# A gated mix of a spectral filter and a squared-relu MLP, forward and backward: ScalarE's order in the opening, and one plain block instead of two in the output pass

## The chip, the core and the metric

The kernel runs on one core of a Trainium2 chip. The core has a matrix engine (TensorE; PE in the profile, PEld its weight loads), a vector engine (VectorE, DVE), a scalar engine (ScalarE, ACT), GpSimd (POOL) and SyncE (SP). Each takes its own instructions in order and waits for others by semaphores. In this kernel SP issues most loads, POOL issues stores and a few loads. The metric is the device time of one execution in microseconds; lower is better. A "profiled execution" is one run recorded by the hardware profiler; its span is the time from the first to the last instruction.

## What is computed

The reference computes an output and, for a given `grad_out`, the gradients of all inputs:

```python
g = sigmoid((x * gate_w).sum(-1, keepdims=True))      # x: 2048 x 1024
a = irfft2(rfft2(x) * (w_r + 1j * w_i))               # spectral branch
b = relu(x @ w1 + b1) ** 2 @ w2 + b2                  # MLP, F = 3584
out = g * a + (1 - g) * b
# and the vjp of this with grad_out, for x, w_r, w_i, w1, b1, w2, b2, gate_w
```

## The kernel before

The matrix work runs in three stages, and a "side" (the two-dimensional transforms of the spectral branch, forward and backward, as small TensorE products with VectorE and ScalarE work around them) is spread between their units.

1. `mlp_in`: for each pair of hidden column blocks and each 512 rows, `hidden` makes `ph` = x w1 (eight matmuls of 128x512), a relu (`rT`, line 748) and its square (`h2T`, line 749) on ScalarE; `grads` makes `pd` = (scaled `grad_out`) w2 transposed (eight matmuls, line 755) and the product with the relu on VectorE (line 759). `h2T` and `dhT` go to DRAM. `ph` and `pd` use few PSUM banks in turn, so a chain can only start when the reader of an earlier one is done.
2. `mlp_grads`: the gradients of w1 and w2.
3. `mlp_out`: the product of the squared relu with w2 (the output rows) and then of `dhT` with w1 (the gradient of x), in blocks of 256 rows.

**The opening.** The first 32 units of stage 1 are written out by a loop (lines 1745 to 1758): units 0 to 7 and 16 to 23 run `hidden`, the others `grads`, and between them tiles of x and of the gradient are transposed (`turn_x`, `turn_grad`) and the gate is made. `weigh` (line 666) gives the row sums `gsum` of one tile of 128 rows on VectorE, as soon as its rows have landed; `gate(i0)` makes the two sigmoids `omg` (1 - g) and `gcol` (g) of four tiles on ScalarE and scales four tiles of the gradient `dbn` by `omg` on VectorE. `gate(12)`, the last, is called after unit 19. From unit 21 on each odd unit takes one step of the side's first stage (`first_stage_of_x`). Its `folds` takes sums and differences of a row on VectorE and copies a few edge elements on ScalarE (lines 263, 265, 269); `row_stage` is the small product `pk`.

The order in which a program's lines are written is not yet the order on an engine: a scheduler sets it from dependencies and its own estimates. `after(ins, earlier, wait)` adds a dependency; with `NoSync` it only fixes the order of two instructions of one engine, with `Sync` (the default) it makes the later one wait.

**The output pass.** `cL` and `cR` are the left and right halves (512 columns each) of w2, 28 blocks of 128 rows; `cL` (tile `w2L`) is loaded earlier, `cR` (tile `w2R`) by seven `rows_of_w2` loads at its start. A block k of 256 rows of the squared relu is loaded by `load("h", k)` into tile `even` or `odd`. A *plain* block makes four chains of 28 matmuls (two row halves by two column halves, tile `acc`, line 1475), each evicted by ScalarE. A *Winograd* block (class `Block`) makes the same by seven chains of 14 matmuls (`p1` to `p7`, line 1378), from sums of quarters: the left sums S1 to S4 of the block (`Block.sums`, VectorE, line 1374) and the right sums T1 to T4 of w2 (`w2_sums`, VectorE, line 1442), made once. Here `p6` reads S2 and T2, `p5` S1 and T1, `p7` S3 and T3, `p4` T4, `p3` S4.

Before, the first two blocks are plain (`N0 = 2`), in the order of `steps`, and blocks 2 to 7 are Winograd blocks. For each output row tile t, `fetch_a` and `fetch_g` load its spectral row and its row of `grad_out`; `prepare` scales the first on ScalarE (`na`) and adds the bias on VectorE (`v`); `close` joins and reduces on VectorE and scales on ScalarE, `put` subtracts and stores. These are kept in a fixed order per engine by `act` and `dve`. The last part of the side, `fft_out`, runs beside the first blocks: its folds (`rf`, VectorE) and copies (`re`, ScalarE) feed its product `pki`, whose result ScalarE copies (`rt`) for the product `pui`.

Of the kernel before, what the change touches and what calls it, by code (L numbers as in the profile page):

```python
# [10 lines left out]
P = 128  # L11
# [4 lines left out]
ACT = mybir.ActivationFunctionType  # L16
# [108 lines left out]
LEAD = 8  # L125
# [15 lines left out]
def kernel(  # L141
# [22 lines left out]
    nc = tc.nc  # L164
# [8 lines left out]
    R1, R2 = g.R1, g.R2  # L173
    NT = S // P
    Q, H, LW, W1 = D // 4, D // 2, g.Df + 1, g.Df
# [6 lines left out]
    ld, st = nc.sync.dma_start, nc.gpsimd.dma_start  # L182
# [7 lines left out]
    go_perm = gof.rearrange("(p t) d -> t p d", t=S2)  # L190
# [17 lines left out]
    gcol, omg, gpg, bGo, dsc = (cols(n, [NT]) for n in ("gcol", "omg", "gpg", "bGo", "dsc"))  # L208
    gsum = cols("gsum", [NT])
# [18 lines left out]
    ax_scr = [[dram.tile([P, D], FDT, name=f"ax_scr{T}_{i}") for i in range(NT)] for T in range(2)]  # L228
# [5 lines left out]
    def after(ins, earlier, wait=mybir.DependencyClass.Sync):  # L234

        if earlier is not None:
            info = mybir.DependencyInfo(wait, mybir.DependencyReason.DATA)
            tc.add_manual_dep(ins.ins, earlier.ins.name, info, reason="paced")


    turn = {"PE": None, "DVE": None, "ACT": None, "copy": None}
# [9 lines left out]
    tps, tps_s = pool("tps", "right", PSUM)  # L251


    def folds(fb, xt, earlier=None):
        uv = fb.tile([P, 2, H], FDT, name="uv", tag="uv", bufs=2)
        after(V(out=uv[:, 0, :], in0=xt[:, 0:H], in1=xt[:, H:D], op=ALU.add), earlier, mybir.DependencyClass.NoSync)
        after(V(out=uv[:, 1, :], in0=xt[:, 0:H], in1=xt[:, H:D], op=ALU.subtract), earlier, mybir.DependencyClass.NoSync)

        f = fb.tile([P, 6, Q + 2], FDT, name="f", tag="f", bufs=2)
        a0, a1 = uv[:, :, 1:Q], uv[:, :, H - 1 : Q : -1]  # L260
        V(out=f[:, 0:2, 1:Q], in0=a0, in1=a1, op=ALU.add)
        V(out=f[:, 2:4, 1:Q], in0=a0, in1=a1, op=ALU.subtract)
        nc.scalar.copy(out=f[:, 3:0:-2, 0], in_=uv[:, 1, 0 : Q + 1 : Q])

        nc.scalar.copy(out=f[:, 0:3:2, 0 : Q + 1 : Q], in_=uv[:, 0:1, 0 : Q + 1 : Q].to_broadcast([P, 2, 2]))
        b0, b1 = f[:, 0:3:2, 0:P], f[:, 0:3:2, Q:P:-1]
        V(out=f[:, 4:6, 0:P], in0=b0, in1=b1, op=ALU.add)
        V(out=f[:, 4:6, P:Q], in0=b0, in1=b1, op=ALU.subtract)
        nc.scalar.copy(out=f[:, 5, P::-P], in_=f[:, 0:3:2, P])
        return f  # L270
# [343 lines left out]

    def rows_of_w2(t_, fc, half, tie=None):
        src = B_w2[fc * P : (fc + 4) * P, half * H : (half + 1) * H]
        after(ld(out=t_[:, fc : fc + 4, :], in_=src.rearrange("(q p) e -> p q e", p=P)), tie)

    db_p, db_s = pool("db")
    dbn = db_p.tile([P, NT, D], BF16, name="dbn", tag="dbn")  # L620
# [4 lines left out]
    later = {}  # L625
    f1, f1_s = pool("f1", "right")

    cf = f1.tile(list(consts["cf"].shape), FDT, name="cf", tag="cf")
    xs = {}
# [42 lines left out]
    def gate(i0):  # L672

        c_ = slice(i0, i0 + 4)
        nc.scalar.activation(omg[:, c_], gsum[:, c_], ACT.Sigmoid, scale=-1.0)
        nc.scalar.activation(gcol[:, c_], gsum[:, c_], ACT.Sigmoid)
        for i in range(i0, i0 + 4):
            later["scaled"] = nc.vector.tensor_scalar(out=dbn[:, i, :], in0=dbn[:, i, :], scalar1=omg[:, i : i + 1], scalar2=None, op0=ALU.mult)
            after(later["scaled"], later["copied"], mybir.DependencyClass.NoSync)

    def first_stage_of_x():
        f, ft = {0: folds(f1, xs[0], later["last"])}, {}
        for i in range(NT + 1):
            if i + 3 < NT:
                xs[i + 3] = source(i + 3, x_perm, later["last"])
            if i < NT:
                ft[i] = row_stage(f1, f[i], kf[:], later["last"])
                yield
            if i > 0:
                first_columns(f1, cf, 0, i - 1, ft[i - 1], later["last"])  # L690
            if i + 1 < NT:
                f[i + 1] = folds(f1, xs[i + 1], later["last"])
            yield
# [23 lines left out]
    def mlp_in():  # L717
# [9 lines left out]
        def bank(name):  # L727
            drawn[0] += 1
            return banks[drawn[0] // 2 % len(banks)].tile([P, SW], FP32, name=name, tag="ph", bufs=2)
# [14 lines left out]
        def hidden(fc, ss, w1g, h2T, rT):  # L744
            ph = bank("ph")
            for dc in range(DC):
                opened(mm(ph[:], lhsT=w1g[:, dc, fc % 2 * P : (fc % 2 + 1) * P], rhs=xT[:, dc, ss], start=(dc == 0), stop=(dc == DC - 1)), fc)  # L747
            nc.scalar.activation(rT[:], ph[:], ACT.Relu, bias=b1col[:, fc : fc + 1])  # L748
            nc.scalar.activation(h2T, rT[:], ACT.Square)  # L749

        def grads(fc, sb, ss, rT, dhT):
            w_ = w2T[fc // FGC]
# [493 lines left out]
    def mlp_out():  # L1246
# [3 lines left out]
        cL, cR, spare = later["w2L"], wr.tile([P, FC, H], BF16, name="w2R", tag="w2R")[:], later["spare"]  # L1250
# [10 lines left out]
        a_, go, na, v, cu, ot, blks, halves = ({} for _ in range(8))  # L1261
# [11 lines left out]
        def load(which, k, issue=ld, tie=None):  # L1273
            t_ = later["odd" if k % 2 else "even"][:, 0 : FC * BW].rearrange("p (c b) -> p c b", b=BW)
            v_ = (h2T_scr if which == "h" else dhT_scr)[:].rearrange("c p s -> p c s")
            for h in (lo, hi):
                after(issue(out=t_[:, h, :], in_=v_[:, h, k * BW : (k + 1) * BW]), tie)
            blks[which, k] = t_
# [5 lines left out]

        def fetch_a(t):
            a_[t] = row("a_", FDT)
            ld(out=a_[t][:], in_=ax_scr[0][t][:])

        def fetch_g(t):
            go[t] = row("go3", BF16)  # L1290
            ld(out=go[t][:], in_=go_perm[t])

        def prepare(t):
            na[t], v[t] = row("na"), row("v")
            act(nc.scalar.mul(out=na[t][:], in_=a_.pop(t)[:], mul=-YS))
            dve(V(out=v[t][:], in0=na[t][:], in1=b2_bc, op=ALU.add))
# [163 lines left out]
            right(T4, cL[:, hi], T2)  # L1460

        blks["h", 0] = later["block"]
        N0 = 2
        fetch_a(0), fetch_g(0), fetch_a(1)
        fetch_g(1)
        made = w2_sums()
        load("h", 1, tie=later["tie"])
        for fc in range(0, FC, 4):
            rows_of_w2(cR, fc, 1)
        steps = [(0, 0), (1, 0), (2, 0), (0, 1), (1, 1), (2, 1), (3, 0), (3, 1)]  # L1470
        for t, hf in steps:
            k, t2 = divmod(t, 2)
            acc = mps.tile([P, H], FP32, name="acc", tag=("pX", "pV")[hf], bufs=2)
            for c in range(FC):
                turn["PE"] = mm(acc[:], lhsT=blks["h", k][:, c, t2 * P : (t2 + 1) * P], rhs=(cL, cR)[hf][:, c, :], start=(c == 0), stop=(c == FC - 1))
            act(nc.scalar.copy(out=fresh(t)[:, (L, R)[hf]], in_=acc[:]))
            turn["copy"] = turn["ACT"]
            if hf:
                if t:
                    put(t - 1)  # L1480
                if t + 1 < 2 * N0:
                    prepare(t + 1)
                close(t)
                fetch_a(t + 2)
                if t + 2 < 2 * N0:
                    fetch_g(t + 2)
                if t == 1:
                    load("h", 2)
            yield 2.0
            n = steps.index((t, hf))  # L1490
            if n == 2:
                prepare(0)
            if 3 <= n < 5:
                next(made)

        wq = iter(())
# [2 lines left out]
            yield from quarter(qs[0], 0, 0)  # L1499
            yield from quarter(qs[1], 0, 1)  # L1500

        a, b = None, Block("h", N0)
        b.sums(3, 1, 2)
        for k in range(N0, NB):
            last = k == NB - 1
            if k == NB - 3:
# [49 lines left out]
            a, b = b, Block("h", k + 1) if not last else Block("d", 0)  # L1556
# [51 lines left out]
        a, b = x1, None  # L1608
        for k in range(2, NB):
            last = k == NB - 1  # L1610
            b = Block("d", k)
# [26 lines left out]
            a = b  # L1638
        a.done = lambda t: close_x(t, ld)
        t_ = 2 * (NB - 1)  # L1640
        c_, v_, o_ = cu.pop(t_), v.pop(t_), row("gxo", BF16, tag="ot")
# [103 lines left out]
    for u in range(32):  # L1745
        for i in before.get(u, ()):
            turn_x(i)
        for i in grads_before.get(u, ()):
            turn_grad(i)
        next(units)  # L1750
        if u in (6, 15, 19):
            gate({6: 4, 15: 8, 19: 12}[u])
        if u == 17:
            for n in range(3):
                xs[n] = source(n, x_perm)
            stage = first_stage_of_x()
        if u > 19 and u % 2:
            next(stage)
    V(out=gpg[:], in0=gcol[:], in1=omg[:], op=ALU.mult)
    later["more_banks"]()  # L1760
# [42 lines left out]
        pass  # L1803
    grads = mlp_grads()
    next(grads), next(grads)
    total = 22 + 2 * (NT + 4) + 14 + 5 + 4 * R1 + 2 + LEAD + 4 * NT
    todo = total - 2 * 12

    def rate():
# [6 lines left out]
    for _ in spread(grads, spec, rate):  # L1816
        pass
    later["side"] = spec
    early = 8 * 2.0 + 3 * 7
    last_rate = (total - count[0]) / (early - 2.0)  # L1820
    for _ in spread(mlp_out(), spec, last_rate):
        pass
# [33 lines left out]
```

## Time and profile before

| | |
|---|---|
| times of four runs | 1205.83, 1207.93, 1207.95, 1210.36 us; median 1207.94 |
| the profiled execution | 1207.95 us, its span 1206.2 us |
| mean TensorE clock granted | 0.998 of full |
| DMA moved | 236.53 MB, mean 196 GB/s |
| TensorE waits in the whole span that the profile names | 4.9 us `ph` for `rT`; 2.0 (5 times) and 0.3 `pki` for `rf`; 1.5 `ph` for `w1g`; 1.2 `pz` for `zeros`; 1.2 `pki` for `re`; 0.5 `pV` for `gxo`; 0.2 `pX` for `u` |

How to read it: a line of a group names the source line, the engine, the operation, the tile written and the tiles read (`out<-in`), the count, then busy time and mean duration in ns, and after the bar the engine's idle time just before these instructions with what ended most of it. A line of a timeline gives start and duration in us, then the instruction, and in brackets the idle time before it and its releaser. `SPq` lines are issues of transfers on SP's queue; the duration is that of the issue, waits included. Matmuls follow each other faster than each one lasts: a group of eight of 128x512 has a duration of about 1.9 us at full clock.

### The profile page before, as it was taken

To read this page: it belongs to the slowest core of one execution; us is meant where nothing else is said; L and a number is where in the kernel's file an instruction comes from. 1 tells how busy PE (TensorE), PEld (TensorE's weight loads), DVE (VectorE), ACT (ScalarE), POOL (GpSimd) and SP (SyncE) were. 2 spreads that over 40 slices of the span, in tenths; PEclk is the share of its full clock that TensorE was granted. 3 is DMA by queue.
4 is the path that set the end of the run, shared out by engine and by line. 5 is a ranking of instruction groups with operands and counts; after the bars stand their busy time and mean duration, and the time that the engine had idled before them with its cause. 6 is when DMAs were issued, how large, how long until landed. Compare 5 with 4: busy or idle time off the path is not lost.

```text
span 1206.2 us, 19779 instructions
## 1 busy us (share of the span) xinstructions
PE 1183.0 (98%) x7055; PEld 648.4 (54%) x7149; DVE 845.3 (70%) x1842; ACT 615.4 (51%) x1121; POOL 366.0 (30%) x587
## 2 busy tenths in 40 slices
PE   9899999999999999999999999999999999999998
PEld 4455545544444444444447888888544544444444
DVE  5765646666879887877789856765489866966464
ACT  6147757855877873444444425554455523232322
POOL 1024424413455550433333353545132100000000
PEclk9999999999999999999999999999999999999999
DMA  9957566575757588999999799986876699965541
GB/s 263 287 170 195 148 201 192 159 171 177 204 175 208 184 224 177 181 213 225 220 201 179 179 234 173 218 199 195 280 215 178 197 206 251 251 194 173 160 150 35
DMA packets 341104, 236.53 MB, mean 196 GB/s; under 512 B 206237, under 2 KB 299963, under 8 KB 341004
## 3 DMA queue, kind: packets, MB, share of 16 engines
q1 hardware_dynamic: 309552, 144.08, 53.6%
q0 software_dynamic: 30224, 90.61, 24.2%
q8 instruction: 56, 0.92, 0.3%
q10 hardware_dynamic: 1228, 0.57, 0.2%
q14 instruction: 44, 0.36, 0.1%
HBM read 107.24 MB, written 81.81 MB: 157 GB/s over the span
## 4 chain that ended last, share of the span: by engine, by line
PE 86%; DVE 5%; DMA 4%; ACT 2%; issue 1%; SPq 1%; ACTq 0%; POOL 0%; DVEq 0%
PE pd L755 15%; PE ph L747 15%; PE pX L1378 13%; PE pV L1378 9%; PE pX L947 8%; PE pX L1023 6%; PE pV L947 6%; PE pV L1023 5%; PE pu L310 2%; PE pk L277 1%; PE px L416 1%; PE pv L447 1%; DMA odd<-h2T_scr 1%; DVE wT L1442 1%; DMA w2R<-in_B_w_dram 1%
## 5 line engine op out<-in xcount | busy, mean ns | idle before, releaser
L747 PE MATMUL ph<-xT,w1g 128*128 128x512 bf16 x867 | 215.8, 381 | 8.1 <-ACT rT L748 4.9
L755 PE MATMUL pd<-dbT,w2T 128*128 128x512 bf16 x876 | 209.5, 379 | 0.9
L755 PEld LDWEIGHTS <-w2T 128*128 128x128 bf16 x896 | 87.2, 98 | 102.8
L747 PEld LDWEIGHTS <-w1g 128*128 128x128 bf16 x896 | 85.7, 98 | 99.9 <-issue 6.8
L759 DVE SCALAR_TENSOR_TENSOR dhT<-pd,rT 128x512 bf16<-128x512 f32 x108 | 74.3, 688 | 77.7 <-PE pd L755 62.6
L748 ACT ACTIVATE rT<-ph,b1col 128x512 bf16<-128x512 f32 x108 | 74.6, 691 | 49.5 <-PE ph L747 46.8
L1023 PEld LDWEIGHTS <-res 128*128 128x128 bf16 (+1 forms) x896 | 86.8, 98 | 11.6 <-issue 0.6
L1378 PEld LDWEIGHTS <-dS 128*128 128x128 f16 x588 | 57.2, 98 | 66.0 <-issue 0.7
L226 POOL DMA_DIRECT2D r<-y_scr x96 | 58.6, 614 | 105.3 <-ACT re L553 57.9
L419 ACT CAST x<-px 64x512 f16<-64x512 f32 x128 | 74.3, 581 | 26.9 <-PE px L416 25.8
L226 POOL DMA_DIRECT2D z_scr<-u x96 | 58.8, 619 | 91.8 <-ACT u L294 47.9
L749 ACT ACTIVATE h2T<-rT 128x512 bf16<-128x512 bf16 x108 | 68.0, 630 | 2.3
L1023 PEld LDWEIGHTS <-X 128*128 128x128 f16 x672 | 64.9, 98 | 7.8
L1378 PEld LDWEIGHTS <-odd 128*128 128x128 bf16 (+1 forms) x392 | 38.2, 98 | 45.3
L1378 PEld LDWEIGHTS <-even 128*128 128x128 bf16 (+1 forms) x392 | 38.1, 98 | 44.2
L456 POOL DMA_DIRECT2D y_scr<-pc x64 | 36.2, 567 | 63.0 <-DVE pc L453 60.2
L947 PEld LDWEIGHTS <-S 128*128 128x128 f16 x336 | 32.8, 98 | 39.7 <-DVE S L921 0.3
L394 POOL COPY w<-wn 128x512 bf16<-128x512 bf16 x32 | 23.9, 746 | 89.4 <-DVE tt L427 73.8
L1351 POOL DMA_DIRECT2D out_dram<-gxo x14 | 7.6, 542 | 131.3 <-DVE gxo L1350 131.3
L1400 DVE TENSOR_TENSOR cu<-pV,u 128x512 f16<-128x512 f32 x27 | 18.6, 690 | 40.9 <-PE pV L1378 34.8
L1378 PE MATMUL pX<-wT,dS 128*128 128x512 f16 x196 | 44.6, 379 | 0.0
L810 POOL DMA_DIRECT2D h2T_scr<-h2T x28 | 20.8, 742 | 77.2 <-ACT h2T L749 43.4
(275 smaller groups left out, 2472.3 us busy)
## 6 DMA issues: line engine op xcount, KB each, us to landing
h2T_scr<-h2T POOLq DMA_DIRECT2D x28, 512.0 KB, 4.2
dhT_scr<-dhT POOLq DMA_DIRECT2D x28, 512.0 KB, 5.2
z<-z_scr SPq DMA_DIRECT2D x64, 128.0 KB, 2.7
y_scr<-pc POOLq DMA_DIRECT2D x64, 128.0 KB, 3.7
ax_scr<-yo POOLq DMA_DIRECT2D x32, 256.0 KB, 5.5
out_dram<-whi POOLq DMA_DIRECT2D x28, 256.0 KB, 4.9
out_dram<-wlo POOLq DMA_DIRECT2D x28, 256.0 KB, 4.8
even<-h2T_scr SPq DMA_DIRECT2D x8, 896.0 KB, 7.1
```

Source lines behind the costliest of these rows:

```text
L226: issue(out=a, in_=b) if stored else issue(out=b, in_=a)
L310: first_ = mm(pu[:, bank, lo : lo + n], lhsT=ft[:, b, :], rhs=mat[:, o : o + n], start=bool(f_ & 1), stop=bool(f_ & 2), skip_group_check=True,
L419: nc.scalar.copy(out=x[lanes[n], c, :, 0:HW], in_=px[lanes[c], n])
L456: st(out=y_scr[:][c, :, :, h].rearrange("r x t l -> (r x) t l"), in_=pc[:, n])
L747: opened(mm(ph[:], lhsT=w1g[:, dc, fc % 2 * P : (fc % 2 + 1) * P], rhs=xT[:, dc, ss], start=(dc == 0), stop=(dc == DC - 1)), fc)
L748: nc.scalar.activation(rT[:], ph[:], ACT.Relu, bias=b1col[:, fc : fc + 1])
L749: nc.scalar.activation(h2T, rT[:], ACT.Square)
L755: opened(mm(pd[:], lhsT=w_[:, ec, fc % FGC * P : (fc % FGC + 1) * P], rhs=dbT[:, ec, ss], start=(ec == 0), stop=(ec == DC - 1),), fc)
L759: return STT(out=dhT, in0=pd[:], scalar=2.0, in1=rT[:], op0=ALU.mult, op1=ALU.mult, accum_out=gb1part[:, fc, sb : sb + 1],)
L947: self.mm = mm(acc[:], lhsT=lhs[:, t, c_], rhs=rhs[:, t, :], start=start and t == 0, stop=t == KH - 1, skip_group_check=True,)
L1023: ins = mm(acc[:, j * FH : (j + 1) * FH], lhsT=lhs[:, t, c_], rhs=rhs[:, t, :], start=start and first_ is None, stop=t == KH - 1, skip_gro ...
L1378: pe(mm(acc[:], lhsT=lhs[:, c, :], rhs=rhs[:, c, :], start=start and c == 0, stop=c == KH - 1, skip_group_check=True,))
```

## The change

In the opening, `omg` and the edge copies of `folds` get an order behind the last square that was written before them (`later["squared"]`); the last gate is called after unit 21 instead of 19, and the side's first step after unit 23 instead of 21. In the output pass there is one plain block (`N0 = 1`), its steps are both left halves and then both right halves; `w2R` is loaded first and the rows of tiles 0 and 1 behind it; block 1 is loaded behind the first chain; T1 is made after the second step, the left sums of block 1 and T2 after the third, T3 and T4 in block 1. The counts that spread the side follow.

```diff
-    def folds(fb, xt, earlier=None):
+    def folds(fb, xt, earlier=None, copies=None):
...
-        nc.scalar.copy(out=f[:, 3:0:-2, 0], in_=uv[:, 1, 0 : Q + 1 : Q])
-
-        nc.scalar.copy(out=f[:, 0:3:2, 0 : Q + 1 : Q], in_=uv[:, 0:1, 0 : Q + 1 : Q].to_broadcast([P, 2, 2]))
+        edge = nc.scalar.copy(out=f[:, 3:0:-2, 0], in_=uv[:, 1, 0 : Q + 1 : Q])
+        after(edge, copies, mybir.DependencyClass.NoSync)
+
+        edge = nc.scalar.copy(out=f[:, 0:3:2, 0 : Q + 1 : Q], in_=uv[:, 0:1, 0 : Q + 1 : Q].to_broadcast([P, 2, 2]))
+        after(edge, copies, mybir.DependencyClass.NoSync)
...
     def gate(i0):
         c_ = slice(i0, i0 + 4)
-        nc.scalar.activation(omg[:, c_], gsum[:, c_], ACT.Sigmoid, scale=-1.0)
+        first_ = nc.scalar.activation(omg[:, c_], gsum[:, c_], ACT.Sigmoid, scale=-1.0)
+        after(first_, later.get("squared"), mybir.DependencyClass.NoSync)
         nc.scalar.activation(gcol[:, c_], gsum[:, c_], ACT.Sigmoid)
...
     def first_stage_of_x():
-        f, ft = {0: folds(f1, xs[0], later["last"])}, {}
+        f, ft = {0: folds(f1, xs[0], later["copied"], later["squared"])}, {}
...
-            nc.scalar.activation(h2T, rT[:], ACT.Square)
+            later["squared"] = nc.scalar.activation(h2T, rT[:], ACT.Square)
...
-        N0 = 2
-        fetch_a(0), fetch_g(0), fetch_a(1)
-        fetch_g(1)
+        N0 = 1
         made = w2_sums()
-        load("h", 1, tie=later["tie"])
         for fc in range(0, FC, 4):
-            rows_of_w2(cR, fc, 1)
-        steps = [(0, 0), (1, 0), (2, 0), (0, 1), (1, 1), (2, 1), (3, 0), (3, 1)]
+            loaded = rows_of_w2(cR, fc, 1)
+        for ins in (fetch_a(0), fetch_g(0), fetch_a(1), fetch_g(1)):
+            after(ins, loaded, mybir.DependencyClass.NoSync)
+        steps = [(0, 0), (1, 0), (0, 1), (1, 1)]
...
-                if t == 1:
-                    load("h", 2)
             yield 2.0
             n = steps.index((t, hf))
+            if n == 0:
+                load("h", 1, tie=turn["PE"])
+            if n == 1:
+                next(made)
+                prepare(0)
             if n == 2:
-                prepare(0)
-            if 3 <= n < 5:
+                b = Block("h", N0)
+                b.sums(3, 1, 2)
                 next(made)
...
-        a, b = None, Block("h", N0)
-        b.sums(3, 1, 2)
+        a = None
...
-        if u in (6, 15, 19):
-            gate({6: 4, 15: 8, 19: 12}[u])
+        if u in (6, 15, 21):
+            gate({6: 4, 15: 8, 21: 12}[u])
...
-        if u > 19 and u % 2:
+        if u > 22 and u % 2:
             next(stage)
...
-    total = 22 + 2 * (NT + 4) + 14 + 5 + 4 * R1 + 2 + LEAD + 4 * NT
+    total = 23 + 2 * (NT + 4) + 14 + 5 + 4 * R1 + 2 + LEAD + 4 * NT
...
-    early = 8 * 2.0 + 3 * 7
+    early = 4 * 2.0 + 4 * 7
```

`rows_of_w2`, `fetch_a` and `fetch_g` now return their load.

More of the change, by code (lines that the diff above doesn't have):

```diff
@@ L616, in rows_of_w2 @@
         src = B_w2[fc * P : (fc + 4) * P, half * H : (half + 1) * H]
-        after(ld(out=t_[:, fc : fc + 4, :], in_=src.rearrange("(q p) e -> p q e", p=P)), tie)
+        loaded = ld(out=t_[:, fc : fc + 4, :], in_=src.rearrange("(q p) e -> p q e", p=P))
+        after(loaded, tie)
+        return loaded
     db_p, db_s = pool("db")
@@ L1286, in fetch_a @@
             a_[t] = row("a_", FDT)
-            ld(out=a_[t][:], in_=ax_scr[0][t][:])
+            return ld(out=a_[t][:], in_=ax_scr[0][t][:])
         def fetch_g(t):
             go[t] = row("go3", BF16)
-            ld(out=go[t][:], in_=go_perm[t])
+            return ld(out=go[t][:], in_=go_perm[t])
         def prepare(t):
```

## The prediction

> **What bounds the kernel now.** I read the page first, then the waits of TensorE over the whole span, then the timelines of the two places that the change touches. The page says that the span is TensorE's:
>
> ```profile
> span 1206.2 us, 19779 instructions
> PE 1183.0 (98%) x7055; PEld 648.4 (54%) x7149; DVE 845.3 (70%) x1842; ACT 615.4 (51%) x1121; POOL 366.0 (30%) x587
> L747 PE MATMUL ph<-xT,w1g 128*128 128x512 bf16 x867 | 215.8, 381 | 8.1 <-ACT rT L748 4.9
> ```
>
> Only 23 us are not TensorE's, so a gain is a matmul left out or one of those waits. The longest is 4.9 us, before a `ph` chain, for a relu. The opening's timelines (start, duration, instruction, idle time before it) show why:
>
> ```profile
> 53.12 0.61 PE L647 MATMUL pt<-identb,dbn 128*128 128x128 bf16 x8
> 58.59 3.41 PE L747 MATMUL ph<-xT,w1g 128*128 128x512 bf16 x8 [4.86 <-ACT rT L748]
> 62.73 1.89 PE L747 MATMUL ph<-xT,w1g 128*128 128x512 bf16 x8
> ...
> 49.43 0.69 ACT L748 ACTIVATE rT<-ph,b1col 128x512 bf16<-128x512 f32 x1 [0.37 <-PE ph L747]
> 55.76 0.20 ACT L675 ACTIVATE omg<-gsum 128x4 f32<-128x4 f32 x1 [5.64 <-DVE gsum L666]
> 55.87 0.19 ACT L676 ACTIVATE gcol<-gsum 128x4 f32<-128x4 f32 x1
> 55.96 0.61 ACT L749 ACTIVATE h2T<-rT 128x512 bf16<-128x512 bf16 x1
> 57.76 0.20 ACT L263 COPY f<-uv 128x2 f16<-128x2 f16 x1 [1.19 <-DVE uv L257]
> 57.86 0.68 ACT L748 ACTIVATE rT<-ph,b1col 128x512 bf16<-128x512 f32 x1
> ```
>
> ScalarE works in order. At 50.1 it reaches the sigmoid of the last four gates, which needs the last row sums (VectorE's line 666, held by rows of x still on their way), and stands until 55.76. Then an edge copy of the first fold waits until 57.76. Only then comes the relu that frees TensorE's bank. The eight matmuls after the stall take 3.41 us, those of the next chain 1.89. The stretches of the clock (length; busy time of PE, PEld, DVE, ACT, POOL; then PE's clock) say why:
>
> ```profile
> 54.88:58.29 3.41, 0.00 (x0) 0.00 (x0) 2.17 (x6) 1.35 (x5) 0.00 (x0) 1.00 1.10 347
> 58.29:61.70 3.41, 3.11 (x8) 1.04 (x8) 3.41 (x11) 1.97 (x6) 0.00 (x0) 0.50 1.16 243
> ```
>
> A stretch without a matmul, then one of the same length at half clock: that costs another 3.41 x 0.5 = 1.70 us.
>
> In the output pass the stretch of the plain rows lasts 55.83 us for 53.94 of TensorE work, and its loads and sums stand thus:
>
> ```profile
> 838.37:894.20 55.83, 53.94 (x306) 26.64 (x311) 31.26 (x77) 24.07 (x40) 13.93 (x24) 1.00 0.81 240
> ...
> 835.37 1.26 SPq L1277 DMA_DIRECT2D odd<-h2T_scr  x2
> 842.93 13.09 SPq L617 DMA_DIRECT2D w2R<-in_B_w_dram  x7
> 871.98 3.89 DVE L1442 TENSOR_TENSOR wT<-w2R,w2L 128x7168 f16<-128x7168 bf16 x1
> 882.23 0.40 PE L566 MATMUL pki<-ki,re 128*128 128x128 f16 x4 [1.17 <-ACT re L553]
> 967.32 6.04 PE pX L1378 x28
> ```
>
> The first sum of w2 starts at 871.98 although `w2R` had landed by 864.3 (issue 853.22 and 11.1 us to land). VectorE is busy 31.26 of these 55.83 us. The last line, from the chain that ended last, gives 28 matmuls as 6.04 us.
>
> **The opening.** What is added is an order behind "the last square" for `omg` and the two edge copies. `gcol`, the second sigmoid, has none. The changed kernel's order on ScalarE shows it: relu, `gcol`, square, relu, square, relu, square, relu, square, `omg`. This `gcol` is the fourth of four, it carries the wait for VectorE, and `omg` later carries none. So the wait has changed its instruction but not its place: ScalarE still stands until 55.76. The row sums end no earlier, because what is ahead of them on VectorE and SP is unchanged. What goes is the second wait. After `gcol` at 55.76 the square starts at 55.87, the relu 0.63 later at 56.50, and TensorE follows 0.73 behind its start (58.59 - 57.86), at 57.23. Gain 58.59 - 57.23 = **1.36 us**; a stall of 3.50 remains. Behind it nothing is late: the next relu ends near 58.6, before TensorE wants that bank at 59.4; `omg` runs near 60.7 and the four scalings of `dbn` start behind it, while the first transposition of them is due at 63.3.
>
> The half clock: with the stretches where they were, 54.88 to 58.29 would now hold 1.06 us of matmuls instead of none. No row shows what a stretch with 69% idle does. Bounds are 0 and **1.70** saved; the wait of 1.55 us at 10.63 (for `w1g`) was followed by full clock, the empty stretch by half. I take 1.70, since only the empty one shows the half clock.
>
> The Trainium skill, "TensorE: Matmul & The Clock Gate", section "Part 1: The HAM clock gate", says the clock halves after an idle window of about 3.4 us and that the windows run freely, unaligned to the kernel. It agrees with the stretch above, and by it a 3.50 us stall would almost never hold a whole window; but it also speaks against the gain, for 4.86 us holds one in only about (4.86 - 3.41) / 3.41 = 4 of 10 executions (an estimate), so the median before may not carry the 1.70, and by it this term would be 0.7 on average.
>
> The first fold step moves from unit 21 to 23 and its edge copies wait for unit 23's square (about 64.85). Copy, copy, two VectorE adds (0.5 us), copy end near 66.0, and the eight `pk` matmuls are now due after the first `pd` chain, near 65.55: **0.45 lost**. One step of the spectral side moves into the later spread: between 100 and 838 no wait of TensorE is above 0.7, so I set 0, with 0.7 on either side.
>
> Sum of the opening: -1.36 - 1.70 + 0.45 = -2.6.
>
> **The output pass.** A plain block is 4 chains of 28 matmuls, a Winograd block 7 of 14: 112 - 98 = 14 matmuls less, half of the 6.04 us above: **3.02 saved**. VectorE gets more: four left sums of 1.08 and three adds of 0.69, 6.4 us, while T1 moves into its idle time near 850. ScalarE's count stays (four evictions each). On SP four loads of rows (1 MB) and the two of block 1 (1.84 MB) move behind seven of `w2R` (3.67 MB).
>
> Loads: `w2R` waits for memory that the last product frees at 838.4. The queues together moved about 350 GB/s when full (843 to 851). With 0.9 MB of stores in flight and 0.5 MB of later stores and loads on POOL's queue, `w2R` has landed near 854, the second row block of `ax` near 857, block 1 near 863 (8 MB at 350 GB/s and 2 us of start). Needs: the last quarter of `w2R` at 856.8, that row at 858.4, block 1 at 864.5. So they just fit.
>
> Walk, from 838.37 as before: both left halves and side work to 851.66, first right half to 857.70. ScalarE evicts it, makes `na` (0.96), then the side's copies; the transform inside the second right half is 0.4 late, then 0.2 and 0.15. VectorE, from that `na` at 859.45: output row 0 and one side unit 5.0, three left sums 3.26, T2 3.80, so T2 ends at 871.55. TensorE reaches the product that reads it at 872.8, so there is no wait. But output row 1 follows on VectorE (3.2 us), and then the fold that the next transform in this product needs: 875.05 against 873.4, **1.6 lost**. T3 ends at 881.65, wanted at 881.4: 0.3, and 0.3 for the fold behind it. T4 is in time; the sums of block 2 end at 896.5 against 896.0: 0.6. New waits sum to 3.5. Those of before that go: 0.44 for the last of `w2R`, 1.17 and 0.27 above 880, and 0.7 between 901 and 917: 2.6. Net +0.9, so the pass gains 3.02 - 0.9 = **2.1**. Bounds: all new waits vanish, 5.6; the loads 3 us later than reckoned (block 1 as slow as `w2R`'s 12.6 us to land), 0.9 lost.
>
> Total -2.6 - 2.1 = -4.7 on the profiled execution, whose span is 1206.2 and whose own time is 1207.95, with 1.8 around it; the median of the four is 1207.94, so no shift is needed: 1207.95 - 4.7 = **1203.3**.
>
> **Rivals.** (1) *The opening gives only the short part*: the clock still halves after 3.5 us, or the median of the four times, which spread over 4.5 us, lacks the half clock. For: the stall that remains is longer than a stretch. Against: 1.06 us of matmuls in the stretch. 1203.3 + 1.7 = 1205.0. (2) *The loads behind `w2R` are 3 us late*: the rows hold ScalarE's evictions, block 1 holds the left sums and T2. For: loads took 9.4 to 12.6 us to land there. Against: fewer bytes are ahead of them than before. 1203.3 + 3.0 = 1206.3. (3) *Slower*: ScalarE stands at the `na` of row 1, and behind it stand the eviction of the side and the copies that TensorE waits for; each us after 858.4 costs one. It decides against the change from 4.7 + 3.6 = 8.3 us late, at 866.7. An issue near 854 and 12.6 us would give 866.6, about 1212. Against: that landing time came with 2.8 MB queued ahead.
>
> **Chances.** Forecast 0.62 (own range 1201.0 to 1204.3), rival 1 0.16, rival 2 0.16, rival 3 0.06. A measurement of this kernel can tell some 0.3% (3.6 us) from no change. The forecast lies below 1204.3, rivals 1 and 2 within the band, rival 3 at or above 1211.6: faster 0.62, same 0.32, slower 0.06. The range reaches from the forecast's lower end to rival 2: 1201.0 to 1206.5.
>
> **What would show it.** In the changed profile: a TensorE wait of 3.4 to 3.6 us near 57.2 for a relu, with `gcol` (not `omg`) behind VectorE's `gsum` at 55.76; no half clock after it; T1 starting near 849; transforms (`pki`) waiting 1 to 2 us for folds near 870; 14 matmuls less. Wrong if the long stall is gone, if a product of block 1 waits for `odd` or for `w2R`, or if TensorE's waits between 838 and 900 exceed 5 us.

## The result and the profile after

| | before | changed |
|---|---|---|
| median | 1207.23 us (62 runs, 1204.86 to 1219.36) | 1209.6 us (42 runs, 1205.68 to 1219.08) |
| ratio to before | | 1.0021, 95% interval 1.0012 to 1.0031 |
| profiled execution | 1207.95 us, span 1206.2 | 1206.12 us, span 1204.3 |

The changed kernel is a little slower, by 0.2%, where 1203.3 us was forecast. Two later series of 12 runs gave 1215.03 us (with two executions, of 1228.82 and 1232.18 us, in a slower state with a lower clock, which the ratio given below leaves out) and 1212.0 us. The profiled execution is one of the shortest of the 42, so its waits tell less than the whole loss. The list of TensorE's waits in it (us in total, times, longest; `...` marks lines left out, and the changed kernel's line numbers are 2 to 6 higher than before's):

```profile
PE pX L1383 <- DVE ev L584: 1.9, 1, 1.9
PE pX L952 <- DVE S L926: 1.4, 1, 1.4
...
PE pd L760 <- DVE dhT L764: 1.3, 4, 0.5
PE pV L952 <- DVE even L926: 1.3, 1, 1.3
...
PE pV L1028 <- DVE wlo L963: 0.9, 1, 0.9
...
PE ph L752 <- ACT rT L753: 0.5, 1, 0.5
```

Three things can be read. The opening's wait for `rT` (L753, was 4.9) is nearly gone. A new wait of 1.9 for `ev` stands in the output pass. And `S`, `dhT`, `even` and `wlo`, 4.9 us together, are waits in stages 1 and 2 between 250 and 670 us, a stretch in which the edit changes no instruction, only when the side's steps come; none of them was in the list of before.

The opening, ScalarE's timeline of the changed kernel (start, busy us, instruction, idle before it and what ended it):

```profile
52.15 0.21 ACT L681 ACTIVATE gcol<-gsum 128x4 f32<-128x4 f32 x1 [2.73 <-DVE gsum L670]
52.26 0.61 ACT L754 ACTIVATE h2T<-rT 128x512 bf16<-128x512 bf16 x1
52.78 0.67 ACT L753 ACTIVATE rT<-ph,b1col 128x512 bf16<-128x512 f32 x1
...
56.68 0.19 ACT L679 ACTIVATE omg<-gsum 128x4 f32<-128x4 f32 x1
```

As forecast, `gcol` and not `omg` stands behind VectorE's `gsum`, the square and the relu follow at once, and no edge copy lies between. In this execution the last row sums came at 52.15 and not at 55.76, so only 0.46 us of TensorE's wait is left.

The output pass, TensorE's timeline, the two waits above 0.4 us behind 868:

```profile
874.77 0.81 PE L1383 MATMUL pX<-wT,dS 128*128 128x512 f16 x3 [1.88 <-DVE ev L584]
896.54 0.82 PE L1383 MATMUL pX<-wT,dS 128*128 128x512 f16 x3 [0.45 <-DVE dS L1379]
```

That is close to the walk of the forecast, with its 1.6 at 875 and 0.6 at 896. The walk had the transform `pki` wait for its fold `rf`; the wait is shown by the product `pX` ahead of it, for `ev`, which VectorE does just before `rf`, and as forecast both stand behind output row 1 there. T1 begins at 850.05 (forecast near 849), and no product of block 1 waits for a load.

So both edited places behave; the stages between them do not. VectorE's timeline at the seam of stages 1 and 2 shows where two of the waits come from, first in the changed kernel:

```profile
458.44 0.69 DVE L764 SCALAR_TENSOR_TENSOR dhT<-pd,rT 128x512 bf16<-128x512 f32 x1 [2.75 <-PE pd L760]
...
459.18 0.42 DVE L441 TENSOR_TENSOR y<-tt 64x512 f16<-64x512 f16 x1
...
460.06 0.69 DVE L455 TENSOR_TENSOR pc<-pv,vc 128x512 f16<-128x512 f32 x1
...
462.14 2.29 DVE L900 TENSOR_TENSOR T<-dbn 128x4096 f16<-128x4096 bf16 x1
```

and the same place before:

```profile
463.10 0.69 DVE L759 SCALAR_TENSOR_TENSOR dhT<-pd,rT 128x512 bf16<-128x512 f32 x1 [2.75 <-PE pd L755]
...
463.72 2.29 DVE L895 TENSOR_TENSOR T<-dbn 128x4096 f16<-128x4096 bf16 x1
```

Before, the first sum of stage 2 (`T`) starts right behind the last eviction of stage 1 (`dhT`). Now six sums of the spectral side (`y` and `pc`, from 459.18 to 462.1) lie between them. The side is one step later, and these six fell behind the last `dhT` instead of ahead of the last six. TensorE then waits 1.25 for `even` at 467.36 and 1.44 for `S` at 470.70.

### The profile page after: what moved, and what is told of

Its sections match the earlier page's. It is cut to its first block, busy times and chain, and to the rows that moved or that the text cites. A ratio compares the mean times of both kernels' runs of the same rounds, so it can differ in the third digit from the quotient of the medians.

```text
span 1204.3 us, 19753 instructions
## 1 busy us (share of the span) xinstructions
PE 1178.6 (98%) x7041; PEld 645.4 (54%) x7135; DVE 852.7 (71%) x1849; ACT 616.3 (51%) x1121; POOL 361.6 (30%) x587
## 4 chain that ended last, share of the span: by engine, by line
PE 80%; DVE 10%; DMA 4%; issue 3%; ACT 2%; SPq 1%; POOL 0%; DVEq 0%; ACTq 0%; POOLq 0%
PE pd L760 14%; PE ph L752 13%; PE pX L1383 13%; PE pV L1383 9%; PE pX L1028 7%; PE pX L952 6%; PE pV L1028 5%; PE pV L952 5%; PE pu L312 1%; PE pk L279 1%; DMA xsrc<-in_A_x_dram 1%; PE pv L449 1%; PE px L418 1%; PE pki L568 1%; DVE even L1773 1%
## 5 line engine op out<-in xcount | busy, mean ns | idle before, releaser
L753 ACT ACTIVATE rT<-ph,b1col 128x512 bf16<-128x512 f32 x108 | 74.6, 691 | 57.2 <-PE ph L752 54.3
L1383 PEld LDWEIGHTS <-dS 128*128 128x128 f16 x630 | 60.9, 98 | 71.6 <-issue 2.7
L1028 PEld LDWEIGHTS <-res 128*128 128x128 bf16 (+1 forms) x896 | 86.7, 98 | 12.4 <-issue 1.6
L1383 PEld LDWEIGHTS <-odd 128*128 128x128 bf16 (+1 forms) x448 | 43.5, 98 | 50.7
L1383 PE MATMUL pX<-wT,dS 128*128 128x512 f16 x210 | 48.3, 379 | 2.3 <-DVE ev L584 1.9
L428 DVE TENSOR_TENSOR tt<-x,w 128x1028 f16<-128x1028 f16 (+1 forms) x32 | 22.2, 695 | 34.6 <-issue 14.3
```

The costliest lines, as they stand in the source:

```text
L428: V(out=tt[:, 0, :, :, 0:W], in0=x[:, :, :, 0:W], in1=w[:, 0:1, 0:W].rearrange("p (o t) l -> p o t l", o=1).to_broadcast([P, 2, 2, W]), op ...
L1028: ins = mm(acc[:, j * FH : (j + 1) * FH], lhsT=lhs[:, t, c_], rhs=rhs[:, t, :], start=start and first_ is None, stop=t == KH - 1, skip_gro ...
L1383: pe(mm(acc[:], lhsT=lhs[:, c, :], rhs=rhs[:, c, :], start=start and c == 0, stop=c == KH - 1, skip_group_check=True,))
```

## The experiments

The runs are counted in the order in which they stand here. All ratios are to the kernel before, run on the same chip in the same series; its medians there were 1207.4 (runs 1 to 4), 1208.14 (5 to 8) and 1208.36 (9 to 11). A ratio is not the quotient of the two medians (for the fourth run that would be 1.006), so a difference of 0.1 or 0.2% between the two is no effect. Theory S: the side starting one step later (`u > 22`, `total = 23`) costs the time between the two edited places. Theory L, the rival: the loads of the output pass that now stand behind `w2R` land late in many executions.

**The output pass alone.** The changed kernel with before's opening and start of the side:

```
-        if u in (6, 15, 21):
+        if u in (6, 15, 19):
...
-        if u > 22 and u % 2:
+        if u > 19 and u % 2:
...
-    total = 23 + 2 * (NT + 4) + 14 + 5 + 4 * R1 + 2 + LEAD + 4 * NT
+    total = 22 + 2 * (NT + 4) + 14 + 5 + 4 * R1 + 2 + LEAD + 4 * NT
```

and without the orders behind "the last square".

> The output pass of the change with the opening and the side's first step of before. Theory S (the side that starts one step later costs the time, at the seam of the first and second stage and behind it): none of that is here, so the new waits in 240 to 700 us are gone; only the 14 matmuls less and the waits walked in the prediction remain: median about 1207.2 - 2 = 1205, spread as before (about 1 us). Theory L (loads behind w2R land late in many executions): median 1209 or more, spread of 3 us like the changed kernel's, long TensorE waits between 836 and 900.

Measured: 1206.25 us (12 runs), ratio 0.9983 (0.9963 to 1.0003). L asked for 1209 or more: it falls.

**The opening alone**, with the later side, and before's output pass (`N0 = 2`, eight steps, the rows' loads ahead of `w2R`).

> The opening of the change (orders, last gate after unit 21, side's first step after unit 23) with the output pass of before. Theory S: slower than before by the waits at the seam (2.7) and behind it (2 to 3) less what the opening gains: about 1209 to 1212, with the changed kernel's spread. Theory L: faster than before by the opening's gain, about 1205, spread about 1 us.

Measured: 1216.76 us (11 runs), ratio 1.006 (1.0034 to 1.0086). The loss is in this half, and it is larger than the 1209 to 1212 that S expected. Its profile (the longest of the 11 executions, 1220.85 us) also has a wait that the first profile of the changed kernel lacked: 5.0 us of the side's product `px` (L418) for the load of its matrix `ab`.

**The changed kernel without the later side:**

```
-        if u > 22 and u % 2:
+        if u > 19 and u % 2:
...
-    total = 23 + 2 * (NT + 4) + 14 + 5 + 4 * R1 + 2 + LEAD + 4 * NT
+    total = 22 + 2 * (NT + 4) + 14 + 5 + 4 * R1 + 2 + LEAD + 4 * NT
```

> The changed kernel with one thing undone: the side's first step after unit 21 as before (and its count 22). Theory S: faster than the changed kernel by some 5 us, about 1203 to 1205, no wait for S or even near 465. Theory L: as the changed kernel, 1209.6.

Measured: 1202.59 us (12 runs), ratio 0.9958 (0.9935 to 0.998), faster than before and 12.4 below the changed kernel in the same series (next run). Two numbers of the edit decide its sign.

**The changed kernel, unedited**, in the same series:

> The changed kernel once more, for a second profiled execution. Both theories: median near 1209.6. If the profiled execution is one of the long ones (1212 and more), its waits show where they lie: theory S in 240 to 700, theory L in 836 to 900; a long wait of the opening (over 3.4 us, half clock behind it) would be a third place.

Measured: 1215.03 us (12 runs), ratio 1.0041 (1.0017 to 1.0064); the 1209.6 that both theories expected was missed by 5.4. Its profile has the wait for `ab` too, 4.7 us.

**The later side alone**, on the kernel before (the two lines above, nothing else):

> The kernel before with only the later start of the side (its first steps from unit 23 instead of 21, and the count of steps one higher); the order on ScalarE in the opening and the output pass are as before. Theory S (the side being one step behind costs the time from there to the end of the second stage): 1213 to 1219 us, with the waits of TensorE for ab, even and S between 435 and 490 us that the changed kernel shows. Rival (the ties of the sigmoid and edge copies cost it, or only both together): 1205 to 1209, and none of these waits.

Measured: 1214.87 us (7 runs), ratio 1.0053 (1.0031 to 1.0075). TensorE's waits in its profile, among others:

```profile
PE px L416 <- DMA ab<-c_ab: 2.3, 1, 2.3
PE pd L755 <- DVE dhT L759: 1.8, 4, 0.7
PE pX L947 <- DVE S L921: 1.4, 1, 1.4
PE pV L947 <- DVE even L921: 1.2, 1, 1.2
```

The orders in the opening and the output pass are not needed for the loss: the shift by itself brings all these waits.

**The later side, caught up before the spread.** The changed kernel with one line more, so that the side starts late but is in step from about 100 us on:

```
     spec = counted()
+    next(spec)
```

> The changed kernel with one extra step of the side taken just before the side is spread over the rest of the first stage. The first step still starts at unit 23; from about 100 us on the side is where it is in the kernel before. Theory S: 1202 to 1205 us, no wait for ab, even or S at the seam of the two stages. Rival (the later first fold in the opening costs it): 1207 or more.

Measured: 1202.81 us (11 runs), ratio 0.9952 (0.9934 to 0.9971), and none of the waits for `ab`, `even`, `S` or `dhT`. So not the later first fold in the opening costs, but the phase that the side keeps afterwards.

**`ab` off SP's queue.** Why does TensorE wait for `ab`? SP's timeline in the third run, whose side is in step:

```profile
421.91 2.82 SPq L181 DMA_TRANSPOSE even<-h2T_scr  x1
424.82 0.53 SPq L380 DMA_DIRECT2D ab<-c_ab  x1
425.40 6.59 SPq L181 DMA_TRANSPOSE even<-h2T_scr  x2
```

and in the tenth run (below), the changed kernel:

```profile
420.58 8.72 SPq L181 DMA_TRANSPOSE even<-h2T_scr  x3
...
430.49 5.34 SPq L181 DMA_TRANSPOSE even<-h2T_scr  x1
435.93 0.52 SPq L380 DMA_DIRECT2D ab<-c_ab  x1
```

In step, `ab` goes out with two of the four transposing loads of stage 2 still behind it; one step later all four are ahead of it, and the issue of each holds SP for 1.9 to 5.9 us in these profiles. Whether `ab` is in time is then a race, in the five profiles with a late side and `ab` on SP:

| profiled execution | SP held by the last transposing load | `ab` issued | lands after | wanted by TensorE | wait | time |
|---|---|---|---|---|---|---|
| changed, first profile | 4.54 | 433.09 | 3.8 | 437.02 | 0.2, weights alone | 1206.12 |
| fifth run (above) | 5.28 | 438.09 | 5.9 | 441.81 | 2.27 | 1214.67 |
| tenth run | 5.34 | 435.93 | 6.7 | 438.64 | 4.00 | 1213.13 |
| fourth run | 5.94 | 435.15 | 7.1 | 437.61 | 4.72 | 1214.84 |
| second run | 5.38 | 439.54 | 7.7 | 442.24 | 5.02 | 1220.85 |

Where `ab` comes late it also takes longer to land: 5.9 to 7.7 us, where it took 4.4 in the kernel before and 5.4 in the third run. In the first row it is issued 0.4 us ahead of POOL's store of `dhT` (512 KB, 433.53), in the fifth run at the same time as it (438.14), in the others 1.0 to 1.2 behind it (434.97, 433.92, 438.58). That the store is what slows it is read from these five only and was not tried. The edit puts the issue on ScalarE; the order on TensorE and VectorE stays as in the changed kernel:

```
-            ld(out=mats[m][:], in_=cten["ab"].ap()[:, m])
+            nc.scalar.dma_start(out=mats[m][:], in_=cten["ab"].ap()[:, m])
```

> The changed kernel, with the side one step late, but the load of ab issued by ScalarE instead of SP, where the transposing loads are ahead of it; the order on TensorE and VectorE is unchanged. Theory A (most of the loss is TensorE's wait for ab, 4.7 us, and the half clock behind it): 1204 to 1208 us, no wait for ab, the waits for even and S (1.2 and 1.4) still there. Theory V (most of it is VectorE's order at the seam of the two stages): 1209 or more.

Measured: 1210.06 us (12 runs), ratio 1.0019 (0.9997 to 1.0041). In its profile (the longest of the 12, 1220.31 us) the wait for `ab` is gone, those for `even`, `S`, `dhT` and `wlo` stay. Theory A's range was missed and theory V's bound met by 1 us; but the changed kernel has no time in this series, so the two stand side by side below.

**Both sigmoids behind the last square**, on the third run's kernel:

```
-        nc.scalar.activation(gcol[:, c_], gsum[:, c_], ACT.Sigmoid)
+        second_ = nc.scalar.activation(gcol[:, c_], gsum[:, c_], ACT.Sigmoid)
+        after(second_, later.get("squared"), mybir.DependencyClass.NoSync)
```

> The changed kernel with the side's start as before (as in the third run) and with the second sigmoid (gcol) ordered behind the last square as well, like omg. If ScalarE's stand at gcol is what still holds the relu in the opening, TensorE's wait there falls from 2.4 us to under 0.6 and the time to 1199.5 to 1201.5 us. Rival (the relu waits for something else by then): the wait stays above 1.5 and the time at 1202 to 1204.

Measured: 1201.26 us (10 runs, 1200.02 to 1203.59), ratio 0.9946 (0.9929 to 0.9962): by its median the fastest kernel here. TensorE's list of waits for 40 to 100 us has one line:

```profile
PE pk L279 <- ACT f L271: 1.6, 1, 1.6
```

The wait for `rT` is gone from the list, so `gcol` was what held the relu. 1.6 us of it come back at `pk`. Its first edge copies run early (56.27 and 56.96), but on VectorE the four scalings of `dbn`, which now start at 57.78, take until 59.4 and stand ahead of the fold's last sums; the last edge copy, which waits for these, comes at 59.89. So not all of the third run's 2.4 is won: 1.3 us by the medians of the two series, 2.1 against before in each, and with runs this few the second could be anything from -0.3 to 4.1 (95%, by resampling the runs).

**Caught up near 335 us**, with the changed kernel and `ab` off SP beside it. The first has the extra step inside the spread, 36 parts ahead of its end:

```
     def first_rate():
         left_[0] -= 1
+        if left_[0] == 36:
+            next(spec)
```

> The changed kernel with the extra step of the side taken not before the spread but within it, near 335 us: up to there the side is one step late as in the changed kernel, from there on it is where the kernel before has it. If the late part (the load of ab near 442, the seam near 465, wlo near 665) carries most of the loss: 1204 to 1206 us, that is 1202.7 plus the waits for dhT between 250 and 285 (1.3 to 2.3 us) that stay. Rival (the early part carries it): 1208 or more.

> The changed kernel, measured beside the runs before and after this one on the same chip: 1209 to 1215 us by its two earlier medians.

> The changed kernel with the load of ab issued by ScalarE once more, now beside the changed kernel itself. Theory A (the wait for ab is a large part of the loss in most executions): 2 to 6 us below the run before. Theory V (VectorE's order carries it, the wait for ab is rare): within 1.5 us of it. Either way 1208 to 1210.5 us, 6 to 8 above the version whose side isn't late.

Measured: caught up near 335 us 1204.49 (ratio 0.9964, 0.9946 to 0.9982); changed 1212.0 (1.0021, 1.0001 to 1.0042); `ab` off SP 1209.5 (1.0004, 0.9978 to 1.0029); 12 runs each. The medians of this series put the loss in three parts: 2.5 us the wait for `ab` (1212.0 - 1209.5), 5.0 what else comes behind 335 (1209.5 - 1204.49: `even`, `S`, `wlo` and `G` are 3.8 of it in the profile, 1.2 is not named), and some 1.5 ahead of 335 (1204.49 lies 3.9 under before, caught up at 100 us 5.3). Single intervals here are 2 us wide on either side. Resampling the runs gives 95% intervals of -0.5 to 4.4, 3.8 to 7.2 and -0.8 to 3.4 for the three, so only the middle part is clear of the noise by the times alone; for the others the waits in the profiles speak, and the share of each wait was not tried by itself.

What the profiles show ahead of 335 is the wait for `dhT`, by the sum over the 16 rows of `dbn`, which VectorE makes between the evictions of stage 1. Before:

```profile
255.45 0.69 DVE L1765 CAST even<-dbn 128x1024 f32<-128x1024 bf16 x1 [3.71 <-DMA z_scr<-u]
256.18 1.23 DVE L1767 TENSOR_TENSOR even<-even,dbn 128x1024 f32<-128x1024 f32 x1
257.32 0.68 DVE L759 SCALAR_TENSOR_TENSOR dhT<-pd,rT 128x512 bf16<-128x512 f32 x1
```

and in the changed kernel:

```profile
253.38 0.69 DVE L1771 CAST even<-dbn 128x1024 f32<-128x1024 bf16 x1 [3.61 <-DMA z_scr<-u]
254.11 2.48 DVE L1773 TENSOR_TENSOR even<-even,dbn 128x1024 f32<-128x1024 f32 x2
256.51 0.68 DVE L764 SCALAR_TENSOR_TENSOR dhT<-pd,rT 128x512 bf16<-128x512 f32 x1
```

Two sums instead of one stand ahead of the first `dhT`. That is 1.2 us more ahead of it, and the next `pd` waits 0.55 at 257.25. From there VectorE takes turns of two and three sums, 7.27 us for two evictions (256.51 to 263.78), where TensorE's four chains take 4 x 1.73 = 6.9, so nothing is made up, and three more waits of 0.2 to 0.4 follow.

## Why the prediction was wrong

**The step that failed**: "One step of the spectral side moves into the later spread: between 100 and 838 no wait of TensorE is above 0.7, so I set 0, with 0.7 on either side." It is worth +7 us alone on the kernel before (1214.87 against 1208.14), 12.4 between the third and fourth runs, and some 8.5 between the third and tenth, each against before in its own series (-4.8 and +3.6). The absence of waits in the old trace was taken for room. It showed that the old order had none to spend: `T` began the instant the last `dhT` ended, `ab` went out ahead of two transposing loads, one sum and not two stood ahead of a `dhT`. The order of the changed kernel on VectorE and SP, around the seam, has all three in it; the forecast read it for ScalarE in the opening only. None of the rivals held this mechanism; the slow one (late loads behind `w2R`) was refuted by the first run.

**Without that step the sum holds.** 1203.3 was forecast; the kernel with the side in step gave 1202.59 and, late but caught up, 1202.81. That it is this close is in part luck: the opening gave about 1 us more than forecast and the output pass about 1 less, and neither miss is clear of the noise.

**Opening, forecast -2.6; measured about -3.7** (third against first run). That `gcol` is hoisted and stands at `gsum`, and that the edge copy's wait goes, was right: TensorE starts 1.36 us after `gcol`'s start in the third run (54.62, 55.98), where 1.47 was forecast. The forecast for `pk`, 0.45, is 0.2 to 0.4. Its stall of 3.50 was too long in every profile (0.35 to 3.19): the row sums end at other times in each, between 52.15 and 57.39. The 1.36 for the edge copy rests on one profile too. In the first run's, with the opening of before, the sums ended at 52.51 and the relu started only at 56.22, behind the edge copy at 56.12; there the copy's wait was the longer one, and taking it away is worth more. One of the signs by which the prediction was to be wrong, a long stall that is gone, thus came true in the first profile (0.46), but it is not why the time was missed.

**The half clock, forecast gone, is not always gone.** In the ninth run, the opening (windows; busy us of TensorE first, its granted clock third from the end):

```profile
52.83:56.24 3.41, 0.55 (x7) 0.30 (x4) 2.91 (x6) 1.64 (x4) 0.00 (x0) 1.00 1.06 379
56.24:59.65 3.41, 3.41 (x14) 1.55 (x12) 0.00 (x0) 1.89 (x4) 0.00 (x0) 0.50 1.29 180
```

A wait of 2.86 us brought it on; so did 3.12 and 3.19 (second and seventh runs), while 2.31 and 2.41 (sixth and third) did not. Rival 1 was thus right for some executions. With the opening of before, all three profiles show the half clock (waits of 4.86, 3.84 and 3.54 us: before, first and fifth runs), where the prediction's estimate, which let only empty stretches count, gave 4 of 10 for the longest of them.

**Output pass, forecast -2.1; measured -1.2** for the first run (1206.25 against 1207.4; its interval reaches from -4.5 to +0.4, so the forecast is neither shown nor refuted). 1.9 at the fold, 0.6 and 0.3 at transforms and 0.5 at `dS` were walked as 1.6, 0.4, 0.2 and 0.6; the two of 0.3 near 881 did not come. The loads of the rows and of block 1 fit; `w2R` itself held the plain block for 0.7 us in the fourth run's profile and 1.4 in the seventh's.

## What to carry to other kernels

An edit that changes when a background stream starts changes its phase against everything behind it, in lines that the diff doesn't show. Where a trace shows no wait, look for what ends last there and how much earlier than needed, before a zero is put down: compare the new order on every queue at each seam of stages, VectorE's and that of the loads behind transposing loads first. If the start must move, give the stream its lost step back in the open, as the one extra step did for 9 us.

## What the runs showed of the hardware

TensorE's clock was halved after stretches that were not empty. The ninth run (above) decides this: its wait of 2.86 us is shorter than the 3.41 us that the half clock lasts, so no stretch of that length around it was without matmuls. The tenth run at the wait for `ab` (same columns):

```profile
440.15:443.56 3.41, 0.92 (x5) 0.46 (x6) 0.87 (x3) 0.28 (x1) 0.00 (x0) 1.00 1.00 295
443.56:446.97 3.41, 3.41 (x10) 1.18 (x9) 1.71 (x5) 2.73 (x5) 0.00 (x0) 0.50 0.32 87
```

27% of the first stretch was matmuls (16% in the ninth run), and the next 3.41 us ran at 0.50 all the same, which makes the 4.00 us of that wait cost about 1.7 more (an estimate: 3.41 x 0.5). The forecast let only an empty stretch count. The Trainium skill, "TensorE: Matmul & The Clock Gate", section "Part 1: The HAM clock gate", speaks of an idle window of about 3.4 us; the length agrees, but the window here needn't be idle throughout.

The issue of a transposing load held SP's queue for 1.9 to 5.9 us (fourth run; it landed 6.5 to 12.3 us after it was issued), and the plain load behind it waited with it: a 128 KB load that in the third run had landed over 4 us before its use became 0.2 to 5.0 us late, in five profiles, by moving behind two more of them.
